# The first batch of a hashed attention with a gated MLP, its hand-written order of work set anew

## The chip, the cores and the metric

The kernel runs on one core of a Trainium2 chip. The metric is the device time of one execution in microseconds, the median of the runs. In the names of the profile, PE is TensorE (matmuls), PEld its weight loads, DVE VectorE, ACT ScalarE, POOL GpSimd, and SP the queue that issues most transfers.

## The reference

Inputs are q, k and v of shape (4 batches, 8 heads, 768 positions, 64), a projection of 64 x 6, and four weight matrices. All is float32.

```python
q_bits = einsum('bhsd,dk->bhsk', q, proj) > 0          # 6 signs for each position
k_bits = einsum('bhsd,dk->bhsk', k, proj) > 0
mask   = (bucket of q_bits)[:, :, :, None] == (bucket of k_bits)[:, :, None, :]
scores = where(mask, q @ k.T / 8, -1e9)
attn   = softmax(scores)                               # with 1e-9 in the denominator
x      = (attn @ v), heads side by side                # 3072 tokens x 512
out    = x + sigmoid(x @ w_res) * ((gelu(x @ w_gate) * (x @ w_val)) @ w_out)
```

The six signs of a position make its bucket number, and a query attends only to keys of its bucket. The MLP widens 512 to 1536.

## The kernel before

**Pairs and chunks.** Two heads of a batch make a pair: p = 0 to 3 in the first batch, 16 in all. The scores of a pair are 768 x 768 for each of two heads; they are cut into nine chunks of 128 x 1024, so that a batch has 36 chunks, "scores 0" to "scores 35". A chunk is three steps. `scores` (line 407) multiplies keys by queries into one of two PSUM buffers `sp`; ScalarE's exponential (line 412) turns it into a bf16 tile `e`; `values` (line 381, "av n" in the order) multiplies `e` by the values and a column of ones and sums into PSUM, eight matmuls of 65 columns. When a head is through, a small matmul (`preset`, line 352) and `finish` (reciprocal and product, lines 332 and 333) give its part of `x_tok`.

**The mask inside the matmul.** Each position's 64 numbers are widened to 71: the 64, six signs of plus or minus one half, and a constant. A match of all six signs adds a large number to the score, and the exponential of the others vanishes. So before a pair's scores its q and k go through these pieces, whose names are those in the order ("1k0" is pair 1, k, head 0):

- `load` (line 78, "ld"; the first pair head by head on line 96, all of them issued by SP).
- "tr": VectorE transposes 32x32 blocks of the loaded tile (line 194).
- "cast": the 64 columns are written in bf16 into one of four tiles `nat` (lines 182, 184 and 186, by engine).
- "hash": fp32 matmuls with the projection. Pair 0 has one piece for each head and side (`hash_one`, line 235). Pair 1 has two pieces over four heads at once, one for each half of the 64 (`hash_heads`, line 253). Pairs 2 and 3 are done together in four pieces (`hashed`, line 206), as are pairs 4 and 5 of the next batch ("hash 4.0" to "hash 4.3").
- "toks": VectorE transposes the sums back to positions (line 259 for pair 1, line 216 for 2 and 3).
- "bits": the signs are written into `nat`, in four instructions of 32 partitions (line 266 for one head of one side, 32x36; line 225 for both heads of one side, 32x72), on VectorE or in turns on GpSimd and VectorE. Pair 0 has its own form on line 243.
- "turn": six transposes on TensorE (line 285) into a PSUM bank, "r" or "f", which `BANK` names.
- "evac": that bank is copied into the tile `aug`, from which scores are made (line 292 on ScalarE, line 294 on VectorE). For pair 0 "a" and "b" are two parts of such a copy.

For the values, "vals_a" copies v in bf16 (line 299) and "vals_s" sums it (lines 307 to 311), both on GpSimd, which also issues the weight loads ("load_w", line 169). "fill" are matmuls on zeros at the start, "spread s" and "spread w" place the projection, and "x 2" transposes a part of `x_tok` for the MLP.

**What sets the order.** No scheduler: every instruction goes to its engine's queue in the order in which the pieces are called, each queue runs in that order, and waits are added where data or a buffer is not ready. For the first batch the pieces stand in one long string, `ORDER`; `WHO` names the engine of a piece where it isn't the default. "work n" issues what a table has for chunk n (loads and values' preparation of the next pairs). After "scores 35" ScalarE loads the table for gelu, the gate and value products of the first batch follow (`gate_val`, lines 426, 445 and 446), with the signs of pairs 4 to 7 between them, and from then on each batch's attention runs in turns with the former batch's output projection (lines 458 and 472). That part isn't touched.

Of the kernel before, what the change touches and what calls it, by code (L numbers as in the profile page):

```python
# [17 lines left out]
def kernel(  # L18
# [20 lines left out]
    T = S // P  # L39
# [24 lines left out]
    e_pool = ctx.enter_context(tc.tile_pool(name="e", bufs=4))  # L64
# [257 lines left out]
    av = {}  # L322
# [207 lines left out]
    def put(name, fn):  # L530
        do[name] = fn

    BANK = {1: "rfrf", 2: "rfrf", 3: "rrfr"}
    G, V, A = nc.gpsimd, nc.vector, nc.scalar
    WHO = {"cast 0k0": A, "cast 0q0": A, "cast 0q1": A, "cast 2k": V, "evac 0k0a": A,
           "evac 0q0": A, "evac 0q1": A, "bits 1q0": (G, V), "bits 1q1": (G, V)}
# [5 lines left out]
    for h in range(2):  # L542
        for e in range(2):
            x = "0%s%d" % ("qk"[e], h)
# [8 lines left out]
            if e == 0:  # L553
                put("evac " + x, lambda h=h, x=x: turned(0, 0, h, WHO.get("evac " + x, V)))
            else:
                put("evac " + x + "a", lambda h=h, x=x: turned(0, 1, h, WHO.get("evac " + x + "a", V), 0, 2))
                put("evac " + x + "b", lambda h=h, x=x: turned(0, 1, h, WHO.get("evac " + x + "b", V), 2, T))
    put("fill b", lambda: fill(2, 256))
    for p in range(1, HP):
        for e in range(2):  # L560
            x = "%d%s" % (p, "qk"[e])
            put("tr " + x, lambda p=p, e=e: tr(p, e))
            put("cast " + x, lambda p=p, e=e, x=x: cast(p, e, WHO.get("cast " + x, G)))
            if p == 1:
                for h in range(2):
                    put("bits %s%d" % (x, h), lambda p=p, e=e, h=h, x=x: bits_head(p, e, h, WHO.get("bits %s%d" % (x, h), ((V,), (G, V))[e])))
            else:
                put("bits " + x, lambda p=p, e=e, x=x: bits(p, e, WHO.get("bits " + x, ((V,), (G, V))[e])))
            for h in range(2):
                y = "%s%d" % (x, h)  # L570
                put("turn " + y, lambda p=p, e=e, h=h, y=y: turn_pe(p, e, h, BANK[p][2 * h + e]))
                put("evac " + y, lambda p=p, e=e, h=h, y=y: turned(p, e, h, WHO.get("evac " + y, V)))
    for i in range(2):
        put("hash 1.%d" % i, lambda i=i: hash_heads(1, i))
    put("toks 1", lambda: tok_heads(1))
    for i in range(4):
        put("hash 2.%d" % i, lambda i=i: hashed((2, 3), i, i + 1))
    put("toks 2", lambda: tokens((2, 3)))
# [60 lines left out]
    def mlp_mm(n):  # L639
# [10 lines left out]
        "tr 0q0, fill a, spread s, hash 0q0, cast 0k0, tr 0k0, cast 0k1, cast 0q0, tr 0q1, "  # L650
        "hash 0k0, bits 0q0, bits 0k0, fill b, turn 0q0, turn 0k0, evac 0q0, tr 0k1, evac 0k0a, "
        "cast 0q1, spread w, hash 0q1, vals_a 0, cast 1k, hash 0k1, cast 1q, "
        "scores 0, tr 1q, evac 0k0b, vals_s 0, bits 0k1, load_v 3, "
        "scores 1, bits 0q1, tr 1k, turn 0k1, "
        "scores 2, turn 0q1, tr 2q, av 0, evac 0k1a, cast 2q, hash 1.0, evac 0q1, evac 0k1b, "
        "scores 3, hash 1.1, av 1, toks 1, bits 1q0, av 2, bits 1k0, "
        "scores 4, bits 1k1, bits 1q1, "
        "scores 5, av 3, turn 1q0, evac 1q0, "
        "scores 6, av 4, vals_a 1, "
        "scores 7, turn 1k0, finish 00, vals_s 1, ld 4q, av 5, evac 1k0, "  # L660
        "scores 8, av 6, load_w 0, tr 2k, "
        "scores 9, tr 3k, tr 3q, av 7, turn 1k1, "
        "scores 10, turn 1q1, evac 1q1, evac 1k1, cast 2k, load_w 1, cast 3k, av 8, "
        "scores 11, ld 4k, cast 3q, av 9, av 10, "
        "scores 12, hash 2.0, vals_a 2, ld 5q, hash 2.1, "
        "scores 13, hash 2.2, hash 2.3, finish 01, av 11, toks 2, "
        "scores 14, av 12, ld 5k, "
        "scores 15, av 13, bits 2q, bits 2k, turn 2q0, "
        "scores 16, evac 2q0, turn 2k0, vals_a 3, work 16, "
        "scores 17, av 14, load_w 2, evac 2k0, finish 10, turn 2q1, vals_s 2, "  # L670
        "scores 18, evac 2q1, av 15, load_w 3, bits 3k, "
        "scores 19, turn 2k1, bits 3q, av 16, av 17, "
        "scores 20, ld 6q, av 18, av 19, evac 2k1, "
        "scores 21, turn 3q0, "
        "scores 22, av 20, ld 6k, evac 3q0, turn 3k0, "
        "scores 23, tr 4q, turn 3q1, evac 3q1, ld 7q, "
        "scores 24, av 21, cast 4k, evac 3k0, av 22, "
        "scores 25, av 23, work 25, "
        "scores 26, cast 4q, vals_s 3, turn 3k1, ld 7k, av 24, "
        "scores 27, tr 5q, evac 3k1, av 25, "  # L680
        "scores 28, tr 5k, tr 4k, cast 5k, work 28, av 26, "
        "scores 29, av 27, cast 5q, tr 7q, "
        "scores 30, hash 4.0, x 2, av 28, tr 6q, "
        "scores 31, hash 4.1, "
        "scores 32, hash 4.2, av 29, "
        "scores 33, hash 4.3, av 30, "
        "scores 34, tr 7k, av 31, tr 6k, work 34, "
# [84 lines left out]
```

## Time and profile before

| | |
|---|---|
| median of 3 runs | 344.62 us (344.42 to 345.3) |
| the profiled execution, its time | 344.05 us |
| its span, first to last instruction | 342.3 us |
| TensorE busy | 337.0 us (98%) |
| ScalarE busy | 208.1 us (61%) |
| VectorE busy | 192.9 us (56%) |
| GpSimd busy | 86.1 us (25%) |
| first exponential of the first batch starts | 9.53 us |
| gelu's table is loaded, after the last exponential of the first batch | 47.07 us |
| granted TensorE clock | 1.00 |

Matmuls are pipelined, so a busy TensorE need not be at its peak: the time from the start of one group to the start of the next says more than the busy share. In a timeline row the columns are the start, the length from the first start to the last end of a merged group, the engine, line and operation, out<-in with shapes and count, and in brackets the idle time of the engine before it with what ended it. Neighbouring instructions of one engine may overlap a little, so a group of n is shorter than n times one.

### The profile page before, as it was taken

The numbers are of one execution on the slowest core, as the hardware profiler recorded it, in microseconds if no ns is written. First come the engines' busy times: TensorE is split into PE (matmuls) and PEld (weight loads), VectorE is DVE, ScalarE is ACT, GpSimd is POOL, SyncE is SP. The second block draws the span as 40 slices with busy tenths as digits, with TensorE's granted clock in tenths as the row PEclk, the third lists the DMA queues.
The fourth block names the chain that finished last, engine by engine and source line by source line (L and its number), as shares of the span: only waits on it lengthen the run. The fifth ranks groups of instructions, "written<-read, shape, count | busy, mean of one in ns | idle before, by whom it ended". The sixth has DMA issues, their size and how long they took to land.

```text
span 342.3 us, 7633 instructions
## 1 busy us (share of the span) xinstructions
PE 337.0 (98%) x3124; PEld 204.6 (60%) x3124; DVE 192.9 (56%) x406; ACT 208.1 (61%) x235; POOL 86.1 (25%) x165
## 2 busy tenths in 40 slices
PE   8999999999999999999999999999999999999995
PEld 5667665665666665655666665656566665665443
DVE  6878847574444876756344775747334444333343
ACT  4889973237999862325999991222999994322220
POOL 3899830370055000170054000242030000000000
PEclk9999999999999999999999999999999999999999
DMA  7979999979386523518467542725431221000012
GB/s 225 377 153 231 308 184 183 162 114 208 123 186 191 159 77 90 110 19 166 105 164 213 181 107 69 132 49 103 82 97 36 56 56 61 3 0 0 33 61 93
DMA packets 69571, 42.50 MB, mean 124 GB/s; under 512 B 47904, under 2 KB 66592, under 8 KB 69536
## 3 DMA queue, kind: packets, MB, share of 16 engines
q1 hardware_dynamic: 63120, 36.77, 42.5%
q0 software_dynamic: 6336, 5.24, 10.6%
q8 instruction: 24, 0.39, 0.5%
q14 instruction: 11, 0.09, 0.1%
q10 hardware_dynamic: 80, 0.00, 0.0%
HBM read 29.36 MB, written 6.29 MB: 104 GB/s over the span
## 4 chain that ended last, share of the span: by engine, by line
PE 94%; ACT 3%; DMA 1%; DVE 1%; issue 0%; SPq 0%; DVEq 0%; ACTq 0%
PE sp L426 37%; PE fps L472 18%; PE sp L407 17%; PE av L381 10%; PE rps L458 6%; PE hs L206 3%; ACT e L412 3%; PE pt L285 1%; DMA ld<-in_q_dram 1%; PE pt L365 1%; PE hs L235 0%; PE av L352 0%; PE hsh L253 0%; PE av L355 0%; DVE o L479 0%
## 5 line engine op out<-in xcount | busy, mean ns | idle before, releaser
L412 ACT ACTIVATE e<-sp 128x1024 bf16<-128x1024 f32 x144 | 143.6, 1026 | 13.1 <-PE sp L407 8.4
L445 ACT ACTIVATE gt<-sp 128x768 bf16<-128x768 f32 x48 | 38.9, 811 | 93.6 <-PE sp L426 93.6
L407 PE MATMUL sp<-aug,aug 71*128 71x256 bf16 (+1 forms) x384 | 85.8, 325 | 0.3 <-ACT e L412 0.2
L472 PE MATMUL fps<-wo,hh 128*128 128x512 bf16 (+2 forms) x300 | 79.3, 370 | 0.0
L446 DVE TENSOR_TENSOR hh<-gt,sp 128x768 bf16<-128x768 bf16 x48 | 45.8, 955 | 52.1 <-PE sp L426 50.0
L426 PE MATMUL sp<-x_sb,wg 128*128 128x512 bf16 (+1 forms) x384 | 70.5, 326 | 0.1
L426 PE MATMUL sp<-x_sb,wv 128*128 128x512 bf16 (+1 forms) x384 | 70.4, 326 | 0.0
L381 PEld LDWEIGHTS <-e 128*128 128x128 bf16 x1152 | 52.7, 97 | 28.9 <-issue 1.2
L381 PE MATMUL av<-va,e 128*128 128x65 bf16 x1152 | 57.6, 193 | 0.0
L426 PEld LDWEIGHTS <-wg 128*128 128x128 bf16 x384 | 37.0, 98 | 26.0 <-issue 1.8
L426 PEld LDWEIGHTS <-wv 128*128 128x128 bf16 x384 | 37.6, 98 | 24.8
L472 PEld LDWEIGHTS <-hh 128*128 128x128 bf16 x300 | 27.5, 97 | 23.2
L407 PEld LDWEIGHTS <-aug 71*128 71x128 bf16 x384 | 29.4, 97 | 10.9 <-issue 1.4
L194 DVE STREAM_TRANSPOSE t<-ld 128x768 f32<-128x768 f32 (+1 forms) x34 | 30.7, 913 | 4.1 <-DMA ld<-in_q_dram 2.2
L307 POOL TENSOR_TENSOR v<-ldv 128x384 f32<-128x384 f32 x16 | 15.9, 996 | 66.5 <-DMA ldv<-in_v_dram 66.5
L184 POOL TENSOR_SCALAR nat<-ld 128x768 bf16<-128x768 f32 x15 | 12.4, 829 | 73.5 <-DMA aug<-nat 73.5
L476 DVE SCALAR_TENSOR_TENSOR o<-th,fps 128x512 f32<-128x512 f32 (+2 forms) x25 | 16.6, 666 | 24.5 <-PE fps L472 20.1
L458 PE MATMUL rps<-wr,x_sb 128*128 128x512 bf16 x96 | 28.1, 378 | 0.0
L332 DVE RECIPROCAL rec<-av 128x6 f32<-128x6 f32 x32 | 6.2, 193 | 32.9 <-PE av L381 31.0
L359 DVE COPY av<-av 128x390 f32<-128x390 f32 x24 | 13.6, 565 | 19.3 <-PE av L355 19.2
L462 ACT ACTIVATE th<-rps 128x512 f32<-128x512 f32 x24 | 14.2, 593 | 16.5 <-PE rps L458 16.5
L225 DVE TENSOR_SCALAR nat<-htp 32x72 bf16<-32x72 f32 x96 | 21.9, 229 | 1.7
(67 smaller groups left out, 209.5 us busy)
## 6 DMA issues: line engine op xcount, KB each, us to landing
ldv<-in_v_dram SPq DMA_DIRECT2D x16, 384.0 KB, 5.1
out_dram<-o SPq DMA_DIRECT2D x23, 256.0 KB, 2.1
ld<-in_q_dram SPq DMA_DIRECT2D x15, 384.0 KB, 5.1
ld<-in_k_dram SPq DMA_DIRECT2D x15, 384.0 KB, 4.5
wg<-in_moe_w_gate_dram POOLq DMA_DIRECT2D x4, 384.0 KB, 6.8
wv<-in_moe_w_val_dram POOLq DMA_DIRECT2D x4, 384.0 KB, 6.8
wo<-in_moe_w_out_dram POOLq DMA_DIRECT2D x3, 512.0 KB, 6.1
wr<-in_moe_w_res_dram POOLq DMA_DIRECT2D x1, 512.0 KB, 11.6
```

What stands on the lines that cost most here:

```text
L194: nc.vector.transpose(t32[p, side][:, sl].rearrange("p c h n -> p (c h n)"), raw[p, side][:, sl].rearrange("p c d -> p (c d)"))
L225: engs[a % len(engs)].tensor_scalar(nat_of(x)[32 * a:32 * a + 32, :, D:D + NBITS], ht[32 * j:32 * j + 32, :, NBITS * a:NBITS * (a + 1)], 0 ...
L307: nc.gpsimd.tensor_add(v3, vs[:, :, 0:3, :], vs[:, :, 3:6, :])
L381: nc.tensor.matmul(av[p, hi][:, qt, :], e[:, off:off + P], va[:, hi, jt, 0:D + 1], start=first, stop=(p >= HP and jt == T - 1), skip_group ...
L407: nc.tensor.matmul(sp[:, off:off + nq * P], ks[0:KA, hi * T + jt, :], qs[0:KA, hi * T + qt0:hi * T + qt0 + nq, :], start=True, stop=True)
L412: nc.scalar.activation(e, sp, AF.Exp, scale=float(ALPHA))
L426: nc.tensor.matmul(sp[:, c0:c1], w[:, kk, bass.ts(m, P)], xs[:, kk, c0:c1], start=(kk == 0), stop=(kk == KM - 1))
L445: nc.scalar.activation(gt, sp[:, 0:S], AF.Gelu)
L446: nc.vector.tensor_mul(hh[:, m, :], gt, ps[1][:, 0:S])
L458: nc.tensor.matmul(rps, x_sb[b][:, kk, t, :], wr[:, kk, :], start=(kk == 0), stop=(kk == KM - 1))
L472: nc.tensor.matmul(fps[:, cs], hh[:, m, bass.ts(t, P)], wo[:, m, cs], start=(m == 0), stop=(m == KF - 1))
L476: nc.vector.scalar_tensor_tensor(o[:, cs], th[:, cs], 1.0, fps[:, cs], op0=ALU.add, op1=ALU.mult)
```

## The change

Only the first batch's order and four tables beside it change; the computation is the same.

- The third and fourth pair (p = 2 and 3) are hashed each by itself, like the second, so that their signs are 32x36 pieces by head. The two hash pieces of a pair now stand together; the four of pairs 4 and 5 stand two and two.
- The first copies of pair 0's q are made in two parts (four of the six blocks, then two), as those of k were.
- Six buffers of `e` instead of four, so that a chunk's values may come up to six chunks behind its scores; in the new order they come up to four behind (av 3 after scores 7), three in the old one (av 29 after scores 32).
- Engines: the cast of 0k0 goes from ScalarE to GpSimd, 0k1 from GpSimd to ScalarE, 1q from GpSimd to ScalarE, 1k and 3q from GpSimd to VectorE, 2k from VectorE to GpSimd; several copies and signs change engine as `WHO` says.
- The order of nearly all pieces before and between the 36 chunks is new, that of loads and weight loads too.

```diff
@@ -61,7 +61,7 @@
     aug_pool = ctx.enter_context(tc.tile_pool(name="aug", bufs=4))
     t32_pool = ctx.enter_context(tc.tile_pool(name="t32", bufs=6))
     va_pool = ctx.enter_context(tc.tile_pool(name="va", bufs=4))
-    e_pool = ctx.enter_context(tc.tile_pool(name="e", bufs=4))
+    e_pool = ctx.enter_context(tc.tile_pool(name="e", bufs=6))
     sm_pool = ctx.enter_context(tc.tile_pool(name="sm", bufs=2))
     sc_ps = ctx.enter_context(tc.tile_pool(name="sc_ps", bufs=2, space=PSUM))
     av_ps = ctx.enter_context(tc.tile_pool(name="av_ps", bufs=2, space=PSUM))
@@ -530,10 +530,12 @@
     def put(name, fn):
         do[name] = fn
 
-    BANK = {1: "rfrf", 2: "rfrf", 3: "rrfr"}
+    BANK = {1: "rffr", 2: "rfrf", 3: "rfrf"}
     G, V, A = nc.gpsimd, nc.vector, nc.scalar
-    WHO = {"cast 0k0": A, "cast 0q0": A, "cast 0q1": A, "cast 2k": V, "evac 0k0a": A,
-           "evac 0q0": A, "evac 0q1": A, "bits 1q0": (G, V), "bits 1q1": (G, V)}
+    WHO = {"cast 0k1": A, "cast 0q0": A, "cast 0q1": A, "cast 1k": V, "cast 1q": A, "cast 3q": V,
+           "evac 0k0a": A, "evac 0k0b": A, "evac 0k1b": A, "evac 0q0a": A, "evac 0q0b": A,
+           "evac 0q1b": A, "evac 2k1": A, "bits 1k1": (G,), "bits 1q1": (G, V), "bits 2k0": (G,),
+           "bits 2k1": (V,), "bits 2q1": (G, V), "bits 3k1": (G,), "bits 3q0": (G, V)}
     put("fill a", lambda: (fill(7), fill(1, 256)))
     put("spread s", lambda: spread(
         lambda a: projs[32 * a:32 * a + 32, :, 32 * a:32 * a + NBITS], (G, A, A, G)))
@@ -551,7 +553,8 @@
             else:
                 put("turn " + x, lambda e=e, h=h: turn_pe(0, e, h))
             if e == 0:
-                put("evac " + x, lambda h=h, x=x: turned(0, 0, h, WHO.get("evac " + x, V)))
+                put("evac " + x + "a", lambda h=h, x=x: turned(0, 0, h, WHO.get("evac " + x + "a", V), 0, 4))
+                put("evac " + x + "b", lambda h=h, x=x: turned(0, 0, h, WHO.get("evac " + x + "b", V), 4, T))
             else:
                 put("evac " + x + "a", lambda h=h, x=x: turned(0, 1, h, WHO.get("evac " + x + "a", V), 0, 2))
                 put("evac " + x + "b", lambda h=h, x=x: turned(0, 1, h, WHO.get("evac " + x + "b", V), 2, T))
@@ -561,21 +564,14 @@
             x = "%d%s" % (p, "qk"[e])
             put("tr " + x, lambda p=p, e=e: tr(p, e))
             put("cast " + x, lambda p=p, e=e, x=x: cast(p, e, WHO.get("cast " + x, G)))
-            if p == 1:
-                for h in range(2):
-                    put("bits %s%d" % (x, h), lambda p=p, e=e, h=h, x=x: bits_head(p, e, h, WHO.get("bits %s%d" % (x, h), ((V,), (G, V))[e])))
-            else:
-                put("bits " + x, lambda p=p, e=e, x=x: bits(p, e, WHO.get("bits " + x, ((V,), (G, V))[e])))
             for h in range(2):
                 y = "%s%d" % (x, h)
+                put("bits " + y, lambda p=p, e=e, h=h, y=y: bits_head(p, e, h, WHO.get("bits " + y, ((V,), (G, V))[e])))
                 put("turn " + y, lambda p=p, e=e, h=h, y=y: turn_pe(p, e, h, BANK[p][2 * h + e]))
                 put("evac " + y, lambda p=p, e=e, h=h, y=y: turned(p, e, h, WHO.get("evac " + y, V)))
-    for i in range(2):
-        put("hash 1.%d" % i, lambda i=i: hash_heads(1, i))
-    put("toks 1", lambda: tok_heads(1))
-    for i in range(4):
-        put("hash 2.%d" % i, lambda i=i: hashed((2, 3), i, i + 1))
-    put("toks 2", lambda: tokens((2, 3)))
+        for i in range(2):
+            put("hash %d.%d" % (p, i), lambda p=p, i=i: hash_heads(p, i))
+        put("toks %d" % p, lambda p=p: tok_heads(p))
     for p in range(HP):
         put("vals_a %d" % p, lambda p=p: vals_a(p))
         put("vals_s %d" % p, lambda p=p: vals_s(p))
@@ -647,44 +643,46 @@
 
 
     ORDER = (
-        "tr 0q0, fill a, spread s, hash 0q0, cast 0k0, tr 0k0, cast 0k1, cast 0q0, tr 0q1, "
-        "hash 0k0, bits 0q0, bits 0k0, fill b, turn 0q0, turn 0k0, evac 0q0, tr 0k1, evac 0k0a, "
-        "cast 0q1, spread w, hash 0q1, vals_a 0, cast 1k, hash 0k1, cast 1q, "
-        "scores 0, tr 1q, evac 0k0b, vals_s 0, bits 0k1, load_v 3, "
-        "scores 1, bits 0q1, tr 1k, turn 0k1, "
-        "scores 2, turn 0q1, tr 2q, av 0, evac 0k1a, cast 2q, hash 1.0, evac 0q1, evac 0k1b, "
-        "scores 3, hash 1.1, av 1, toks 1, bits 1q0, av 2, bits 1k0, "
-        "scores 4, bits 1k1, bits 1q1, "
-        "scores 5, av 3, turn 1q0, evac 1q0, "
-        "scores 6, av 4, vals_a 1, "
-        "scores 7, turn 1k0, finish 00, vals_s 1, ld 4q, av 5, evac 1k0, "
-        "scores 8, av 6, load_w 0, tr 2k, "
-        "scores 9, tr 3k, tr 3q, av 7, turn 1k1, "
-        "scores 10, turn 1q1, evac 1q1, evac 1k1, cast 2k, load_w 1, cast 3k, av 8, "
-        "scores 11, ld 4k, cast 3q, av 9, av 10, "
-        "scores 12, hash 2.0, vals_a 2, ld 5q, hash 2.1, "
-        "scores 13, hash 2.2, hash 2.3, finish 01, av 11, toks 2, "
-        "scores 14, av 12, ld 5k, "
-        "scores 15, av 13, bits 2q, bits 2k, turn 2q0, "
-        "scores 16, evac 2q0, turn 2k0, vals_a 3, work 16, "
-        "scores 17, av 14, load_w 2, evac 2k0, finish 10, turn 2q1, vals_s 2, "
-        "scores 18, evac 2q1, av 15, load_w 3, bits 3k, "
-        "scores 19, turn 2k1, bits 3q, av 16, av 17, "
-        "scores 20, ld 6q, av 18, av 19, evac 2k1, "
-        "scores 21, turn 3q0, "
-        "scores 22, av 20, ld 6k, evac 3q0, turn 3k0, "
-        "scores 23, tr 4q, turn 3q1, evac 3q1, ld 7q, "
-        "scores 24, av 21, cast 4k, evac 3k0, av 22, "
-        "scores 25, av 23, work 25, "
-        "scores 26, cast 4q, vals_s 3, turn 3k1, ld 7k, av 24, "
-        "scores 27, tr 5q, evac 3k1, av 25, "
-        "scores 28, tr 5k, tr 4k, cast 5k, work 28, av 26, "
-        "scores 29, av 27, cast 5q, tr 7q, "
-        "scores 30, hash 4.0, x 2, av 28, tr 6q, "
-        "scores 31, hash 4.1, "
-        "scores 32, hash 4.2, av 29, "
-        "scores 33, hash 4.3, av 30, "
-        "scores 34, tr 7k, av 31, tr 6k, work 34, "
+        "fill a, spread s, cast 0k0, tr 0q0, tr 0k0, tr 0q1, hash 0q0, spread w, cast 0q0, "
+        "hash 0k0, fill b, bits 0q0, turn 0q0, cast 0q1, bits 0k0, cast 1q, hash 0q1, evac 0q0a, "
+        "tr 0k1, evac 0q0b, turn 0k0, vals_a 0, bits 0q1, tr 1q, hash 0k1, evac 0k0a, evac 0k0b, "
+        "cast 0k1, ld 4k, "
+        "scores 0, vals_s 0, load_v 3, "
+        "scores 1, bits 0k1, cast 1k, tr 1k, turn 0k1, turn 0q1, evac 0q1a, "
+        "scores 2, vals_a 1, tr 2q, av 0, av 1, evac 0k1b, "
+        "scores 3, hash 1.0, hash 1.1, cast 2q, cast 2k, evac 0k1a, toks 1, av 2, bits 1k0, "
+        "bits 1q0, evac 0q1b, bits 1q1, "
+        "scores 4, "
+        "scores 5, bits 1k1, turn 1k0, "
+        "scores 6, tr 2k, turn 1q0, evac 1q0, "
+        "scores 7, evac 1k0, av 3, av 4, finish 00, load_w 0, "
+        "scores 8, load_w 1, av 5, load_w 2, "
+        "scores 9, turn 1q1, tr 3q, turn 1k1, "
+        "scores 10, evac 1k1, av 6, vals_s 1, av 7, evac 1q1, "
+        "scores 11, vals_a 2, ld 4q, av 8, "
+        "scores 12, cast 3q, cast 3k, finish 01, av 9, av 10, "
+        "scores 13, hash 2.0, hash 2.1, tr 3k, toks 2, bits 2k1, "
+        "scores 14, bits 2k0, av 11, "
+        "scores 15, av 12, ld 5q, load_w 3, bits 2q1, av 13, "
+        "scores 16, turn 2k0, bits 2q0, av 14, av 15, vals_s 2, evac 2k0, work 16, turn 2q0, "
+        "scores 17, av 16, evac 2q0, turn 2k1, "
+        "scores 18, turn 2q1, finish 10, evac 2q1, "
+        "scores 19, vals_a 3, ld 5k, av 17, ld 6k, evac 2k1, hash 3.0, hash 3.1, "
+        "scores 20, toks 3, bits 3q0, ld 6q, ld 7q, bits 3k0, "
+        "scores 21, av 18, bits 3q1, cast 4q, turn 3q0, "
+        "scores 22, tr 4k, av 19, evac 3q0, av 20, bits 3k1, "
+        "scores 23, av 21, turn 3k0, "
+        "scores 24, evac 3k0, turn 3q1, vals_s 3, "
+        "scores 25, tr 4q, tr 5q, tr 5k, work 25, turn 3k1, "
+        "scores 26, av 22, "
+        "scores 27, av 23, av 24, "
+        "scores 28, evac 3k1, evac 3q1, work 28, ld 7k, av 25, av 26, "
+        "scores 29, av 27, "
+        "scores 30, hash 4.0, hash 4.1, "
+        "scores 31, tr 6k, cast 4k, av 28, av 29, "
+        "scores 32, tr 6q, hash 4.2, cast 5q, hash 4.3, "
+        "scores 33, x 2, tr 7q, tr 7k, "
+        "scores 34, av 30, cast 5k, work 34, av 31, "
         "scores 35, av 32, av 33"
     )
     chunk = {}
```

## The prediction

> **What bounds the kernel now.** I read the page first, then the timelines of ScalarE, TensorE, VectorE and GpSimd over the first 52 us, then the transfers issued there. From the page:
>
> ```profile
> span 342.3 us, 7633 instructions
> PE 337.0 (98%) x3124; PEld 204.6 (60%) x3124; DVE 192.9 (56%) x406; ACT 208.1 (61%) x235; POOL 86.1 (25%) x165
> ...
> PE 94%; ACT 3%; DMA 1%; DVE 1%; issue 0%; SPq 0%; DVEq 0%; ACTq 0%
> ```
>
> TensorE bounds the whole, but the change touches only the first batch, where ScalarE's 36 exponentials (one per chunk) fill the time nearly as well. What counts is when the last of them ends, since all that follows keeps its order. The timeline of ScalarE (start, duration, name, count, idle before):
>
> ```profile
> 3.78 0.94 ACT L182 ACTIVATE nat<-ld 128x384 bf16<-128x384 f32 x2
> 7.27 1.08 ACT L292 ACTIVATE aug<-pt 71x768 bf16<-71x768 bf16 x2 [2.55 <-PE pt L285]
> 8.24 0.52 ACT L182 ACTIVATE nat<-ld 128x384 bf16<-128x384 f32 x1
> 9.53 2.85 ACT L412 ACTIVATE e<-sp 128x1024 bf16<-128x1024 f32 x3 [0.77 <-PE sp L407]
> 12.26 0.81 ACT L292 ACTIVATE aug<-pt 71x768 bf16<-71x768 bf16 x1
> ...
> 24.85 5.64 ACT L412 ACTIVATE e<-sp 128x1024 bf16<-128x1024 f32 x6 [0.55 <-PE sp L407]
> 30.82 10.30 ACT L412 ACTIVATE e<-sp 128x1024 bf16<-128x1024 f32 x11 [0.34 <-PE sp L407]
> 41.62 2.03 ACT L412 ACTIVATE e<-sp 128x1024 bf16<-128x1024 f32 x2 [0.49 <-PE sp L407]
> ```
>
> Exponentials follow each other every (10.30 - 1.03)/10 = 0.92 us. From the first (9.53) to the last (two from 45.11, so 46.03) are 36.5 us: 35 x 0.92 = 32.2, one PSUM copy (12.26 to 12.95) 0.7, and about 3.6 of waiting, always for scores (line 407). The list of waits names no exponential that waits for a values matmul; a buffer `e` was never short.
>
> How a wait comes about: there are two score buffers, so scores n start at the earliest when exponential n-2 has ended, 1.07 us after that one's start (scores at 10.60, exponential at 9.53); exponential n starts 0.63 us after scores n do (14.31 against 13.68). 2 x 0.92 - 1.07 - 0.63 leaves 0.14 us of play. A chunk's scores occupy TensorE 0.43 us, so other work of 0.92 - 0.43 + 0.14 = 0.63 us fits between two chunks; what is beyond it, ScalarE waits. Prices of that other work, start to start in the timeline of TensorE: values of a chunk 0.25, six transposes 0.34, hash groups as follows.
>
> ```profile
> 23.11 0.86 PE L206 MATMUL hs<-t,projw 128*32 128x192 f32 x16
> 23.90 0.42 PE L381 MATMUL av<-va,e 128*128 128x65 bf16 x8
> ...
> 42.45 0.53 PE L206 MATMUL hs<-t,projw 128*32 128x192 f32 x8
> 42.92 0.42 PE L381 MATMUL av<-va,e 128*128 128x65 bf16 x8
> ```
>
> A hash piece alone takes 0.56 with its entry from the scores (scores at 41.92, their end at 42.35, next work at 42.92); a group of two pieces 0.90 (22.57 + 0.43 = 23.00 to 23.90).
>
> **1. The start: 0.65 later.** ScalarE's new order before the first exponential: casts of 0q0 and 0q1, the cast of 1q, copies of q in two parts, of k in two parts, cast of 0k1. The cast of 1q waits for its load, and the queue is in order, so the first copy (7.27 before) waits with it. That load is the fifth that SP issues, in both kernels, at 2.67, and the view of transfers says
>
> ```profile
> ld<-in_q_dram SPq DMA_DIRECT2D x1, 384.0 KB, 4.7
> ```
>
> so it lands at 7.4. A cast of 768 columns does not occur on ScalarE before. Bounds: 0.72 us of its queue (the 811 ns of `gt`, also 768 columns, less the 0.09 by which neighbours overlap) and 0.86 (two casts of 384, 0.43 start to start). I take 0.80, near the casts. The copies: 768 + 256 columns take 0.97 (7.27 to 8.24), the new 1536 columns 1.46. Cast of 0k1: 0.43. First exponential: 7.45 + 0.80 + 1.46 + 0.43 + 0.04 (a semaphore) = 10.18 against 9.53. TensorE isn't later: its first scores need the first part of k, 7.45 + 0.80 + 0.97 x 1.2 = 9.41, and the exponential could go 0.63 later, at 10.04. Range of this term 0.57 to 0.71.
>
> [...]
>
> The split of the copies hides nothing new, since both parts are on ScalarE ahead of the first exponential. That VectorE is spared its 0.41 us copy at 8.39 gains nothing: its next users wait for hashes.
>
> **2. Copies between exponentials: 0.75 later.** Now three: second part of 0k1 (512 columns, 0.49), second part of 0q1 (256, 0.26), 2k1 (768, 0.70), 1.45 in all, for one of 0.70 before. All stand in the exponentials' own queue; only where ScalarE would wait anyway do they cost nothing (see 20 below).
>
> **3. Hash pieces together: waits of 3.6 become 2.45.** Three groups fewer, each 2 x 0.56 - 0.90 = 0.22 of TensorE. What matters is where they fall. By the rule of 0.63, with what the timeline shows before, new figures in order:
> - exponential 4: waited 0.45 (a hash piece and two chunks of values ahead of scores 4). Now a group and one chunk of values, but the exponentials themselves come later by 0.65 + 0.49, so nothing: 0.
> - 11: 0.25 before, behind transposes, values and a preset (0.34 + 0.25 + 0.17). Now two chunks of values stand there (0.50): 0.
> - 13 and 14: two groups of 0.90 in neighbouring slots, waits 0.41 and 0.65. Now the third pair's group alone, behind scores 13: 0.90 - 0.63 plus some lateness, 0.4.
> - 17 and 18: new, 0.85, worked out below.
> - 20: 0.44 before. The fourth pair's group falls here, but ScalarE copies 2k1 just then: 0 beside the 0.70 already counted.
> - 31 to 34: four lone pieces, waits 0.62, 0.09, 0.33, 0.33. Now two groups: 0.90 - 0.63 = 0.3 and, behind two chunks of values, 0.5.
> - small ones of 0.05 to 0.1: 0.4.
>
> **The new wait at 17.** The third pair's signs are now made head by head in 32x36 pieces: 16 instructions a pair, where two pairs together had 16 of 32x72, and those of 2k0 are all on GpSimd. From GpSimd's timeline:
>
> ```profile
> 14.11 3.16 POOL L266 TENSOR_SCALAR nat<-hth 32x36 bf16<-32x36 f32 x8
> ```
>
> with the next start at 17.34, so 0.40 each. On TensorE the transposes of 2k0 stand after scores 16, and behind them values 14 and 15, the transposes of 2q0 and scores 17. If scores 13 start at time t, the group ends at t + 0.43 + 0.90, with its drain 0.25 and the transpose to tokens 0.38 the signs start at t + 2.0, GpSimd is through at t + 3.65, and then come 0.34 + 0.50 + 0.34 and 0.63 to exponential 17: t + 5.5. Undisturbed it would start at t + 0.7 + 4 x 0.92 + the 0.4 at 14 = t + 4.8. So 0.7, and 0.15 more at 18, where the copy of 2q0 is late. GpSimd must be free by then: 14.5 + eight signs 3.2 + three weight issues (0.98, 0.89, 0.85 in this trace) + sums 2.05 + values copy 0.95 + cast 0.82 = 24.2, and the signs want it at about 24.3. Just so; its cover is nil.
>
> [...]
>
> **4. What I put at nothing.** The buffers of `e` and values further behind: no exponential waited for them; they let 3 happen. Loads: 4k and 4q issue earlier, 5q and 5k follow the first transposing DMA of `x_sb` (22.5 before), those of pairs 6 and 7 the second (31.5, as before); 12 us and 9 us later their transposes read them, and the longest landing of these early loads is 8.5. The cast of 0k0 goes to GpSimd, which is idle from 3.6 to 6.1 and needs 0.50. The banks r and f alternate in both orders. The third weight slice (46.4) comes some 2 us later and is wanted six gate blocks after 46.4, at 2.45 each near 61. VectorE takes two casts instead of one and about 0.5 us more of signs; it idles over 6 us of these 38. TensorE idles 0.8 us before the first scores; the granted clock is 1.00 throughout, so I price no slow matmuls.
>
> **Sum.** 0.65 + 0.75 + (2.45 - 3.6) = +0.25 us. The profiled execution took 344.05 around its span of 342.3; it becomes 344.3. The median of the runs is 0.57 above it: 344.62 + 0.25 = 344.9.
>
> **Rivals.**
> - Slower, decided at GpSimd's signs of the third pair. If GpSimd finishes its cast of 3k after 24.3, every microsecond is one at scores 17, and ScalarE has nothing later to make it good. With the 0.55 of its 32x72 signs in place of 0.40, twelve signs (eight of the second pair, four of these) give 12 x 0.15 = 1.8: 344.9 + 1.8 = 346.7; half of it 345.8. For it: zero cover, signs of both engines at once. Against: the same form measured 0.40 beside VectorE.
> - Faster: neither the start nor 17 waits. If the load of 1q came 0.65 earlier and the signs were ready with the transposes, 0.65 + 0.85 go: 343.4. Against: the loads ahead of it are unchanged and 4.7 us is measured.
> - It does nothing: the exponentials are paced by scores alone, and moved work only changes which slot waits: 344.6. For it: both engines have under 4 us of slack, and my terms nearly cancel.
>
> **How the numbers follow.** A measurement of this kernel tells 0.3%, 1.03 us, from no change. My sum and the third rival lie within it: 0.62 together (0.47 and 0.15). The slower rival and mishaps on its path beyond 1.03: 0.24. The faster rival: 0.14. Range: without the wait at 17 and with the low start price, 344.9 - 0.85 - 0.1, and a little toward the faster rival, 343.6; above, three quarters of the GpSimd rival, 346.2.
>
> **What would show it.** First exponential near 10.2, behind a ScalarE cast that waits for a load; a wait of 0.7 before the 18th; last exponential starting near 46.3. The prediction is wrong if the first exponential starts by 9.6, if exponential 17 waits not at all or over 1.5 us, or if the stages after 48 us change in length.

## The result and the profile after

The changed kernel takes 345.40 us (median of 22 runs, 344.70 to 348.86) against 344.49 for the one before (22 runs, 343.93 to 345.30): a ratio of 1.0031, 95% interval 1.002 to 1.0042. It is slower by 0.91 us; forecast were 0.25 more, 344.9, with a range of 343.6 to 346.2. The difference lies under the 1.03 us that the prediction takes for the limit of one measurement; over 22 runs the interval still excludes no change.

The profiled execution of the changed kernel is the one of 348.86 us, so it must be read with care. From its page, beside the lines shown of before:

```profile
span 347.1 us, 7643 instructions
PE 339.9 (98%) x3124; PEld 206.6 (60%) x3124; DVE 192.8 (56%) x412; ACT 210.1 (61%) x240; POOL 87.9 (25%) x173
...
PEclk9679999999999999999999999999999999999999
...
PE 92%; ACT 3%; DMA 2%; SPq 0%; DVE 0%; issue 0%; DVEq 0%; ACTq 0%
```

The second and third digit of PEclk are new (before had 9 throughout), and so is the 1% more of DMA on the chain that ended last. ScalarE's timeline shows both (start, length, engine, line, operation, shapes, count, idle before):

```profile
5.06 0.52 ACT L182 ACTIVATE nat<-ld 128x384 bf16<-128x384 f32 x1 [0.81 <-DMA ld<-in_q_dram]
8.24 0.84 ACT L182 ACTIVATE nat<-ld 128x768 bf16<-128x768 f32 x1 [2.65 <-DMA ld<-in_q_dram]
8.99 1.60 ACT L292 ACTIVATE aug<-pt 71x512 bf16<-71x512 bf16 x4
10.47 0.53 ACT L182 ACTIVATE nat<-ld 128x384 bf16<-128x384 f32 x1
10.88 1.94 ACT L412 ACTIVATE e<-sp 128x1024 bf16<-128x1024 f32 x2
...
17.59 1.94 ACT L412 ACTIVATE e<-sp 128x1024 bf16<-128x1024 f32 x2 [1.56 <-PE sp L407]
19.99 1.02 ACT L412 ACTIVATE e<-sp 128x1024 bf16<-128x1024 f32 x1 [0.47 <-PE sp L407]
21.49 1.02 ACT L412 ACTIVATE e<-sp 128x1024 bf16<-128x1024 f32 x1 [0.47 <-PE sp L407]
```

The cast of 1q holds ScalarE for 2.65 us, until its load lands at 8.24 (7.41 in the profile before, issued at 2.67 in both). Then exponentials follow each other only every 1.5 us. TensorE's timeline and its table by stretches say why (in the table: stretch, its length, busy time of PE, PEld, DVE, ACT and POOL with counts, granted clock, DMA share, GB/s):

```profile
7.67 0.87 PE L235 MATMUL hs<-t,projs 128*128 128x192 f32 x4
10.16 1.04 PE L407 MATMUL sp<-aug,aug 71*128 71x512 bf16 x5 [1.62 <-ACT aug L292]
...
18.20 0.85 PE L285 MATMUL pt<-ident,nat 128*71 128x128 bf16 x6
```

```profile
0.00:11.90 11.90, 9.21 (x55) 6.04 (x56) 8.85 (x24) 6.62 (x14) 5.19 (x20) 1.00 0.79 256
11.90:22.10 10.20, 10.15 (x82) 6.26 (x81) 5.92 (x16) 7.28 (x10) 7.72 (x18) 0.50 0.74 244
22.10:46.00 23.90, 23.60 (x366) 17.10 (x365) 20.05 (x50) 22.59 (x25) 19.74 (x42) 1.00 1.09 233
```

After 1.62 us without work TensorE's granted clock fell to one half from 11.9 to 22.1; six transposes take 0.85 there, 0.50 to 0.53 elsewhere. From first to last exponential this run needs 39.61 us, and the same order at full clock 36.48 (below): 3.1 us. But it is one run of 22; the others have a mean clock of 0.997 to 1.0, and half clock for 3.41 us (a third of this stretch) would already give 0.995 (an estimate, over 347 us). The half clock explains the slowest run, not the median.

### The profile page after: what moved, and what is told of

It is laid out like the page before. It is cut to its first block, busy times and chain, and to the rows that moved or that the text cites. A ratio compares the mean times of both kernels' runs of the same rounds, so it can differ in the third digit from the quotient of the medians.

```text
span 347.1 us, 7643 instructions
## 1 busy us (share of the span) xinstructions
PE 339.9 (98%) x3124; PEld 206.6 (60%) x3124; DVE 192.8 (56%) x412; ACT 210.1 (61%) x240; POOL 87.9 (25%) x173
## 4 chain that ended last, share of the span: by engine, by line
PE 92%; ACT 3%; DMA 2%; SPq 0%; DVE 0%; issue 0%; DVEq 0%; ACTq 0%
PE sp L426 36%; PE fps L472 18%; PE sp L407 18%; PE av L381 10%; PE rps L458 6%; PE hs L206 2%; ACT e L412 2%; DMA ld<-in_q_dram 2%; PE pt L285 1%; PE hsh L253 1%; ACT aug L292 1%; PE pt L365 1%; SPq L96 0%; PE av L352 0%; ACT nat L182 0%
## 5 line engine op out<-in xcount | busy, mean ns | idle before, releaser
L407 PE MATMUL sp<-aug,aug 71*128 71x256 bf16 (+1 forms) x384 | 88.3, 334 | 1.7 <-ACT aug L292 1.6
L184 POOL TENSOR_SCALAR nat<-ld 128x768 bf16<-128x768 f32 x13 | 11.6, 891 | 73.8 <-DMA aug<-nat 73.7
```

Source lines behind the costliest of these rows:

```text
L407: nc.tensor.matmul(sp[:, off:off + nq * P], ks[0:KA, hi * T + jt, :], qs[0:KA, hi * T + qt0:hi * T + qt0 + nq, :], start=True, stop=True)
```

## The experiments

All kernels from here on are stand-ins: the transposing DMAs are replaced by plain copies, and later batches' scores use the first batch's q and k, so the later batches' result is left out. The stand-in of after takes as long as after itself, 345.42; that of before takes 1.0 us more than before. Steps that wait for no load repeat within 0.02 us between profiles of one order; the landing of loads does not repeat (that of 1q, issued in its place, came between 6.97 and 8.24). "Exponential n" is the start of the n-th, and a step is the time from one start to the next, both read from the single instructions.

```diff
-        ag = aug_pool.tile([P, HT, P], BF16, tag=f"aug{side}", name=f"aug{side}")
-        nc.sync.dma_start_transpose(out=ag, in_=nat_of(x).rearrange("p c n -> p (c n)"))
+        ag = aug[p % HP, side]
+        nc.sync.dma_start(ag[KA:P].rearrange(...), nat_of(x)[KA:P].rearrange(...))
```

**The two orders at full clock.**

> A stand-in for the kernel before, as a basis for the experiments: its 35 transposing DMAs are replaced by plain copies on the same queue at the same places. Those of x_tok copy it as it is; those of pairs 4 to 15 copy the unused rows of nat into the unused rows of the first batch's transposed tiles, and the later batches take q and k from the first batch. So the later batches' result is left out, while the instructions of every compute engine are those of the kernel before, in its order. Expected by every theory: the first batch as before (first exponential 9.5, last one 46.0), a time within 1 us of 344.5.

> The same stand-in for the changed kernel. Expected by every theory: 0.9 us above the stand-in for the kernel before, as the changed kernel is above it. Theory of the start: its first exponential starts past 10.1, behind ScalarE's cast of 1q that waits for its load, and this is most of the 0.9 us. Theory of the slots: the first exponential is late by 0.65 at most and waits between the exponentials make the rest. Theory of the clock: TensorE's granted clock falls to 0.50 for a stretch after its idle time ahead of the first scores, as in the first profile of the changed kernel (0.50 from 11.9 to 22.1 us after 1.62 us of idling), and typical runs pay for that in part.

Measured: stand-in of before 345.5 (345.25 to 345.78), ratio to before 1.0032 (1.0019 to 1.0044); of after 345.42 (344.47 to 346.2), 1.0028 (1.0019 to 1.0038). In the former the values of pair 0 reached GpSimd at 9.35 instead of 8.56, and step 6 was 1.49 instead of 0.90, a wait for signs; the other 0.4 lies behind exponential 35 (296.68 against 296.31), where before's profile is the shortest of all. So the stand-in of after is compared with the profile of before itself, at clock 1.00 both:

| | before | prediction's change | stand-in of after | measured change |
|---|---|---|---|---|
| load of 1q landed | 7.41 | 0 | 6.97 | -0.44 |
| exponential 0 | 9.53 | +0.65 | 9.61 | +0.08 |
| 0 to 4 | 4.78 | -0.40 | 4.46 | -0.32 |
| 4 to 6 | 1.83 | 0 | 1.82 | -0.01 |
| 6 to 14 | 8.71 | -0.91 | 7.82 | -0.89 |
| 14 to 18 | 3.70 | +0.85 | 5.17 | +1.47 |
| 18 to 30 | 11.53 | +0.26 | 11.95 | +0.42 |
| 30 to 35 | 5.95 | -0.57 | 5.26 | -0.69 |
| behind 35 | 296.31 | 0 | 296.62 | +0.31 |

(The prediction's 0.4 of small waits has no place of its own.) From 0 to 35 before took 36.50 and after 36.48: all that is gained up to 14 and behind 30 is used up between, most of it at exponential 17. The 0.31 behind 35 falls almost all in the last 55 us, in the stand-in of before as well (54.58 there, 54.59 here, 54.27 before), so it isn't taken for the change's. What is left is the start.

**Does the start hang on that load?** Cast of 1q taken off ScalarE in after, and put there in before:

```diff
-"cast 1q": A, ... bits 0k0, cast 1q, hash 0q1 ... tr 2q, av 0
+             ... bits 0k0, hash 0q1 ... tr 2q, cast 1q, av 0        # on VectorE
```

> The stand-in for the changed kernel with one cast moved: 1q goes to VectorE, behind tr 2q, so that nothing on ScalarE waits for that load ahead of the first copies. Theory of the start: the first exponential starts near 9.5 and the end moves by as much, 0.6 to 1.3 us down from the stand-in for the changed kernel. Theory of the slots: what is won at the start is lost in the waits after it, 0.2 at most is left. Theory of the clock: TensorE's idle time ahead of the first scores falls under 0.6 us and the clock stays at 1.00.

> The stand-in for the kernel before with one part of the change: the cast of 1q on ScalarE ahead of the first copy, where it waits for its load. Theory of the start: the first exponential moves from 9.5 to 10.1 or later; the end is later by 0.4 to 1.0 us, as some is given back by GpSimd's relief and by waits that the delay covers. Theory of the slots: under 0.3 later.

```diff
-load(1, 0); load_v(0); load(1, 1)
+load_v(0); load(1, 1); load(1, 0)
```

> The stand-in of after with the load of 1q issued two places later on SP, behind the values of pair 0 and behind 1k, so that it lands near 9.5 instead of 7.0 to 8.2. ScalarE's cast of 1q then holds the first copies, the first exponential should start near 12.1 (landing + 2.64), and TensorE idles some 3 us before the first scores. Theory clock (TensorE idle for 1.6 us or more there is followed by a granted clock of one half for several windows of 3.4 us): rows of 0.50 in the windows after 12 us, steps of 1.5 in place of 0.95 between early exponentials, 3 to 4 us beyond the late start; time 349 to 351. Rival start (a late load only shifts the start): clock 1.00, first exponential 2.5 later, and part of it covered by later waits; time 346.5 to 347.9.

Measured: 345.45 (345.42 to 345.63), 345.34 (344.59 to 346.38) and 349.21 (347.31 to 350.56). ScalarE's timeline of the last:

```profile
9.42 0.84 ACT L182 ACTIVATE nat<-ld 128x768 bf16<-128x768 f32 x1 [3.54 <-DMA ld<-in_q_dram]
10.17 1.60 ACT L292 ACTIVATE aug<-pt 71x512 bf16<-71x512 bf16 x4
11.65 0.53 ACT L182 ACTIVATE nat<-ld 128x384 bf16<-128x384 f32 x1
12.06 2.85 ACT L412 ACTIVATE e<-sp 128x1024 bf16<-128x1024 f32 x3
```

In every profile with after's order the first exponential starts 2.64 after the cast of 1q: 6.97 and 9.61, 7.57 and 10.22, 8.24 and 10.88, 9.42 and 12.06. And lateness is handed on whole: with starts at 9.61 and 12.06 exponentials 0 to 35 took 36.48 each. Earliness is not: with the cast on VectorE the start was 9.29, but the stretch took 37.49, since VectorE's copies and GpSimd's signs came later (step 4 1.79, step 6 1.05). GpSimd's timeline in the stand-in of after, then with the cast on VectorE:

```profile
8.10 0.82 POOL L299 CAST va<-ldv 128x768 bf16<-128x768 f32 x1 [2.88 <-DMA ldv<-in_v_dram]
...
14.00 3.20 POOL L266 TENSOR_SCALAR nat<-hth 32x36 bf16<-32x36 f32 x8
```

```profile
8.63 0.82 POOL L299 CAST va<-ldv 128x768 bf16<-128x768 f32 x1 [3.34 <-DMA ldv<-in_v_dram]
...
14.53 3.20 POOL L266 TENSOR_SCALAR nat<-hth 32x36 bf16<-32x36 f32 x8
```

So a second chain hangs on the next load of SP's queue, the values of pair 0: from their copy to its signs of pair 1 GpSimd needs 5.90 both times, hardly pausing, and exponential 6 comes 7.79 after that copy both times. The copy starts 1.11 to 1.15 after the landing of 1q in the five profiles that show both. By that, 8.63 stands for a landing at 7.50 (an estimate), and the cast on ScalarE would have given 7.50 + 2.64 + 6.28 = 16.42 for exponential 6 (6.28 is the stretch from 0 to 6 in the stand-in of after), which is where it came without it. The two chains are level, and taking the cast away shortens only one.

In before's order the cast on ScalarE cost 0.59 at the start (10.08) and 0.21 at exponential 35; as the copy of the values started at 9.35 without it and at 8.70 with it, the 0.21 is not its price at equal loads. Neither median moved as the theory of the start had it (345.45 against 345.42, 345.34 against 345.5).

**Does the idle stretch halve the clock?** Zeros on TensorE ahead of the first scores, with the late load:

```diff
-hash 0k1, evac 0k0a
+hash 0k1, fill c, evac 0k0a          # fill c: ten matmuls of 512 columns on zeros
```

> As the kernel with the late load of 1q, and ten matmuls on zeros (512 columns each, about 0.21 us at full clock) behind the hash of 0k1 on TensorE, so that it idles about 1 us instead of 3 before the first scores, which don't come later by that. Theory clock: the granted clock stays 1.00, steps of early exponentials are 0.95 again, and the time is 346.5 to 347.9, 3 us less than without the zeros. Rival (the clock does not hang on that idle stretch): same clock and same time as without the zeros.

Measured 348.08 (347.77 to 349.16). With the late load alone the four runs had mean clocks of 0.999, 0.995, 0.99 and 0.985 at 347.31, 348.87, 349.55 and 350.56: 3.25 us over 1.4%, or 1.2 for each half per cent. A third of after's stretch at half clock, 3.41 us, would be 0.5% of the span (an estimate). But a later landing lengthens both the idle stretch (none with the landing at 6.97, 1.62 at 8.24, 2.03 at 9.42) and the time, and the landings of these runs aren't known, so not all of the 3.25 need be the clock's. With the zeros the clocks were 1.0, 1.0, 0.998 and 0.995, and the median missed the 346.5 to 347.9 that was expected. Both profiles show 1.00 in the whole first batch (0.999 and 1.0 over the span); in the one with zeros 1q landed at 10.64, 1.2 later than in the other, so their times can't be set against each other. Three runs of four with lost clock against one or two speak for the theory, but don't show it; what the zeros gain stays open.

**Who is late at exponential 17?** One piece moved in GpSimd's queue:

```diff
-scores 12, cast 3q, cast 3k, finish 01 ... evac 2q1,
+scores 12, cast 3q, finish 01 ... evac 2q1, cast 3k,        # behind scores 18
```

> The stand-in of after (transposing DMAs replaced by plain copies, so that the later batches' result is left out), with one piece moved: GpSimd's cast of 3k goes from behind scores 12 to behind scores 18, so that it no longer stands ahead of the third pair's four signs in GpSimd's queue. In the stand-in of after that cast ended at 24.22 while the tokens were ready at 23.52, and exponential 17 waited 1.41 (step 2.33). Theory GpSimd (its lateness sets the wait at 17): the signs start about 0.7 earlier, the step at 17 falls to 1.6, and the last exponential comes 0.7 earlier; time 344.7 against 345.4. Rival hash (the chain from the hash group through tokens and signs sets it): the step at 17 stays above 2.2 and the time at 345.4. Rival slots (time won at 17 is lost again in later waits): step 17 near 1.6, but the steps from 18 to 35 give it back, time 345.3.

Measured 345.11 (344.39 to 345.92), ratio 1.0018 (1.0007 to 1.0028). GpSimd's timeline in the stand-in of after, and below it TensorE's:

```profile
23.41 0.81 POOL L186 CAST nat<-ld 128x768 bf16<-128x768 f32 x1
24.32 1.61 POOL L266 TENSOR_SCALAR nat<-hth 32x36 bf16<-32x36 f32 x4
```

```profile
25.98 0.53 PE L285 MATMUL pt<-ident,nat 128*71 128x128 bf16 x6 [0.59 <-POOL nat L266]
```

GpSimd's timeline with the cast of 3k moved:

```profile
23.97 0.14 POOL L300 MEMSET va<- 128x12 bf16 x1
24.30 1.53 POOL L266 TENSOR_SCALAR nat<-hth 32x36 bf16<-32x36 f32 x4 [0.19 <-DVE hth L259]
```

In the first the cast ends at 24.22, the tokens were ready at 23.52, and the transposes of 2k0 wait. In the second GpSimd waits for the tokens; the step at 17 falls from 2.33 to 1.63, and the stretch from 0 to 35 from 36.48 to 35.77. The 0.7 is GpSimd's and lasts to the end; the median gains 0.31, and which landings its runs had isn't recorded. After's own profile shows the same from the other side: at half clock the hash came late, GpSimd idled 1.56 before these signs, and the step at 17 was 1.62.

**Hash pieces together, alone** (in the stand-in of before):

```diff
-cast 2q, hash 1.0, evac 0q1, evac 0k1b, scores 3, hash 1.1, av 1
+cast 2q, evac 0q1, evac 0k1b, scores 3, hash 1.0, hash 1.1, av 1
-scores 30, hash 4.0, ... scores 31, hash 4.1, scores 32, hash 4.2, av 29, scores 33, hash 4.3
+scores 30, ... scores 31, hash 4.0, hash 4.1, scores 32, av 29, scores 33, hash 4.2, hash 4.3
```

> The stand-in of before with one part of the change alone: the two hash pieces of pair 1 stand together behind scores 3, and the four of pairs 4 and 5 stand two and two behind scores 31 and 33. By the prediction's prices the waits at 31 to 34 fall from 1.37 to 0.8 and the one at 4 from 0.45 to about 0.6, since both pieces now stand ahead of scores 4. Theory slots (a group of two costs 0.22 less than two alone and the exponentials gain what TensorE saves): last exponential 0.4 to 0.5 earlier than in the stand-in of before, time 345.0 against 345.5. Rival nothing: the wait only changes its slot, time 345.5. A time above 345.8 speaks against both.

Measured 344.76 (344.04 to 345.25), ratio 1.0006 (0.9996 to 1.0017), 0.74 below the stand-in of before (in the profiles 0.30 of that is an earlier start, 9.19 against 9.49). ScalarE's timeline with the pieces apart, then together:

```profile
42.17 2.03 ACT L412 ACTIVATE e<-sp 128x1024 bf16<-128x1024 f32 x2 [0.49 <-PE sp L407]
44.42 1.02 ACT L412 ACTIVATE e<-sp 128x1024 bf16<-128x1024 f32 x1 [0.22 <-PE sp L407]
45.67 1.94 ACT L412 ACTIVATE e<-sp 128x1024 bf16<-128x1024 f32 x2 [0.23 <-PE sp L407]
```

```profile
42.54 1.94 ACT L412 ACTIVATE e<-sp 128x1024 bf16<-128x1024 f32 x2 [0.30 <-PE sp L407]
44.79 1.94 ACT L412 ACTIVATE e<-sp 128x1024 bf16<-128x1024 f32 x2 [0.31 <-PE sp L407]
```

Waits of 0.3 twice (the prices were 0.3 and 0.5) in place of four; exponentials 30 to 35 took 5.47 instead of 5.97. Step 4 fell too, 1.37 to 1.22.

**Can both costs be taken away?** Cast of 1q on GpSimd and 2k's behind scores 8; then also 3k's and two weight issues behind scores 18:

```diff
-bits 0k0, cast 1q, hash 0q1 ... scores 0, vals_s 0 ... cast 2q, cast 2k ... scores 8, load_w 1
+bits 0k0, hash 0q1 ... scores 0, cast 1q, vals_s 0 ... cast 2q ... scores 8, cast 2k, load_w 1
```

> The stand-in of after with the cast of 1q taken off ScalarE and given to GpSimd, behind the copy of pair 0's values, so that the first exponential no longer hangs on the landing of 1q; to keep GpSimd's signs of pair 1 in time, its cast of 2k goes from behind scores 3 to behind scores 8. Theory start (from exponential 0 to exponential 35 the stand-ins of after with the first exponential at 9.61, 12.06 and 13.29 all took 36.48, so a start earlier is an end earlier, one for one): first exponential at 9.2 to 9.5, last one 36.5 later at 45.9, and a median 0.5 to 0.9 below the 345.4 of after's stand-in: 344.6 to 344.9. Rival cover (what is won at the start is waited for later, as when the cast went to VectorE, where 36.48 became 37.49): last exponential at 46.5 or later, time 345.4.

> As the kernel with the cast of 1q on GpSimd, and the third pair's signs freed too: GpSimd's cast of 3k goes behind scores 18, and so do its third and fourth weight issue, which stood ahead of and between the third pair's signs. Theory start and GpSimd together (they add: 0.9 at the start, 0.7 at exponential 17): first exponential at 9.2 to 9.5, step at 17 of 1.6, last exponential at 45.1, median 343.8 to 344.2, below both kernels (344.5 and 345.4). Rival (only one of the two gains lasts): 344.6 to 344.9. Rival weights (the weight slices now come too late for the first gate blocks): last exponential at 45.1 and yet a time above 344.6, with the stage behind 46 us longer than in after's stand-in.

Measured 346.05 (345.64 to 346.69) and 345.7 (344.78 to 347.75): slower than after's stand-in. Two more, set by those traces: 2q's cast behind the signs too, and the weight issues at scores 25; and, with GpSimd as it was but for 3k, the cast of 1q on ScalarE ahead of exponential 4.

```diff
-evac 0q1b, bits 1q1
+evac 0q1b, cast 1q, bits 1q1        # the second of the two; cast 1q gone from ahead of hash 0q1
```

> As the kernel with both moves on GpSimd (cast of 1q there, cast of 3k behind scores 18), with two things set right that its trace named: the cast of 2q goes behind GpSimd's signs of pair 1, since the transposes of 1k0 waited 0.58 for those signs (step at exponential 6 1.29 in place of 0.90), and the third and fourth weight issue go to scores 25, since exponential 22 waited 0.7 for the signs of 3k0 behind them (step 1.63). Theory GpSimd (what was won at the start was lost only where GpSimd's queue came late): signs of pair 1 start 0.7 earlier, steps at 6 and 22 fall to 0.90 and 0.95, step 17 stays 1.63, last exponential near 45.5, median 344.0 to 344.4. Rival loads (the landings of 1q, the values and 1k set when the signs of pair 1 can be made, whichever engine is free): exponential 6 not before 16.3 and last one at 46.1 or later; median 344.8 to 345.5.

> The stand-in of after with GpSimd's cast of 3k behind scores 18, and the cast of 1q still on ScalarE but later, behind the second part of 0q1's copy and ahead of exponential 4, so that no work ahead of the first exponentials waits for the load of 1q, and GpSimd has nothing more to do. Theory start (only the hang on the landing costs): first exponential at 9.2 to 9.5, 0.75 of cast ahead of exponential 4, of which up to 0.4 hides under the wait that pair 1's signs make at 6; exponential 6 near 16.3, step 17 at 1.6, last exponential near 45.8, median 344.2 to 344.6 with less scatter than the 344.4 to 345.9 of the kernel with 3k moved alone. Rival loads (a start before the loads allow is waited for at 6): exponential 6 near 16.5 in any case, last one at 46.0 or later, median 344.9 to 345.2.

Measured 344.64 (343.67 to 345.33), ratio 0.9999 (0.9986 to 1.0011), and 344.84 (344.46 to 345.86), 1.0013 (1.0002 to 1.0024). TensorE's timeline, cast on GpSimd alone:

```profile
16.30 0.53 PE L285 MATMUL pt<-ident,nat 128*71 128x128 bf16 x6 [1.36 <-DVE nat L266]
```

and with GpSimd's queue set anew:

```profile
15.03 0.53 PE L285 MATMUL pt<-ident,nat 128*71 128x128 bf16 x6 [0.65 <-POOL nat L266]
```

These are the transposes of 1k0. Starts were at 9.42, 9.80, 9.22 and 9.32; exponential 6 came at 17.36, 16.52, 16.08 and 16.39 (15.89 in after's stand-in): pair 1's signs, not the first exponential, set the pace there, and they hang on the values of pair 0, whose copy started at 9.74, 8.91, 9.17 and 8.73 (8.10 in after's stand-in). The four kernels got 0 to 35 in 38.80, 37.04, 36.93 and 36.57. Step 17 was 2.82, 1.62, 2.06 and 1.62; the second lost its gain at exponential 22 (step 1.63 in place of 0.95, signs of 3k0 behind the weight issues), which the third mended. The fourth pays for the cast at exponential 4 (step 1.90 in place of 1.27). All four medians lie above what the theory gave. Part of that is loads: after's own order, with a copy of the values as late, would end 37.99 behind it (46.09 less 8.10; an estimate), and against this the last exponentials of the four come 0.49 later, then 0.06, 1.01 and 0.83 earlier. Their medians, against 345.42, lie 0.63 and 0.28 higher, 0.78 and 0.58 lower. The third is 0.8 below after's stand-in and level with before; none beats both kernels clearly.

## Why the prediction was right or wrong

The time lay in the range and on the right side of no change, but 0.5 above the sum. One term was clearly mis-sized, the wait at 17 (3 and 4); one was near, but stood on a landing that doesn't repeat (1).

1. **The start.** Price of the cast (0.80) and order were right: it measured 0.84, of which 0.75 is queue time. At the landing of 7.41 the rule of 2.64 gives 10.05, so +0.52 and not +0.65, just under the bound of 0.57. What failed is "so it lands at 7.4": a fixed landing, taken from one execution. In the four profiles with this cast on ScalarE and the load in its old place it landed at 6.97, 7.57, 7.57 and 8.24. Lateness goes to the end one for one, since 36.48 followed the starts at 9.61, 12.06 and 13.29. At 7.41 the last exponential would come at 10.05 + 36.48 = 46.53, 0.50 behind before's 46.03; against the stand-in of before, at its later loads, the same sum gives 0.75 (both estimates). The medians differ by 0.91. The rest is open: runs without a profile don't show their landings, and the stretch behind 35 alone took 296.31 to 297.12 over the profiles.
2. **Copies between exponentials and waits up to 14** were right: -0.40 and -0.91 predicted, -0.32 and -0.89 measured.
3. **The wait at 17** was mis-sized: 0.7 predicted, 1.41 at full clock. The 0.7 is what the chain through hash, tokens and signs costs alone (step 1.63 with 3k moved). "Just so; its cover is nil" was the point that decided: GpSimd came free at 24.22, as worked out (24.2), but the tokens were there at 23.52 and not at 24.3, and the 0.70 that it was late is the 0.70 more at exponential 17. The drain of 0.25 in that chain stands in no row: the transpose to tokens began 0.14 after the work behind the hash group on TensorE in before (23.90 to 24.04), 0.13 in the stand-in of after (23.01 to 23.14). A later start doesn't mend it: the step was 2.33 with the late load as well, for the reason under 4. So the slower rival's mechanism holds, with 0.7 in place of 0.9 to 1.8; its price was wrong in kind, since the signs kept their 0.40 and the lateness came from the queue ahead of them.
4. **VectorE beside GpSimd.** VectorE's ten signs took 2.59 (1.95 with 3k moved), and the transposes of 2k0 waited 0.59 for GpSimd's signs, not for these. But the change also gave VectorE the cast of 3q, and that lengthened a GpSimd addition ahead of the signs. Of GpSimd in after's stand-in, the addition beside that cast, and a later one without:

```profile
20.12 1.41 POOL L307 TENSOR_TENSOR v<-ldv 128x384 f32<-128x384 f32 x1
...
27.72 0.99 POOL L307 TENSOR_TENSOR v<-ldv 128x384 f32<-128x384 f32 x1
```

and of VectorE:

```profile
20.13 0.55 DVE L184 TENSOR_SCALAR nat<-ld 128x768 bf16<-128x768 f32 x1
```

   With the late load GpSimd reached that addition 0.52 sooner after the first exponential, and it took that much longer:

```profile
22.05 1.94 POOL L307 TENSOR_TENSOR v<-ldv 128x384 f32<-128x384 f32 x1
```

```profile
22.58 0.55 DVE L184 TENSOR_SCALAR nat<-ld 128x768 bf16<-128x768 f32 x1
```

   In seven of the eight stand-ins in which the two overlap, the addition ends 0.85 or 0.86 after the cast does, whenever it began; in the eighth the cast took 1.17 instead. So it is VectorE's new cast that fixes when GpSimd comes to the signs, and with the late load less work ahead of the addition won nothing. Of GpSimd's 0.70 it makes 0.42 in the stand-in of after; with the late load it makes 0.95, without which GpSimd would have come before the tokens and the 0.7 of the sum would have held (worked out from the rows; no run takes the cast of 3q off VectorE). The failed step is the one that put VectorE's second cast at nothing. In six of the eight the addition had begun first and was still the one that took longer (1.41 and 1.94 in the rows above, 0.99 without the cast beside it); what holds it up, no run shows.
5. **31 to 34** were right: two waits of 0.3 in the stand-in of before; 30 to 35 -0.69 against -0.57 in after's.
6. **"I price no slow matmuls"** was wrong as a rule, though it hardly moves the median: it costs 3.1 us in the run where it happens.
7. What else was put at nothing (buffers, later loads, weights) shows no wait of an exponential. The "does nothing" rival is near in outcome and wrong in reason: the stretch from 0 to 35 is 36.48 against 36.50 because +1.89 (14 to 30) and -1.91 (the other stretches) cancel. That is luck, and so is part of the hit: the start at 7.41 (0.13 less than priced), 30 to 35 (0.12 less) and the 0.4 of small waits, for which the other stretches leave about 0.25, stand against 0.62 more at 14 to 18.

The stated marks: exponential 0 near 10.2 behind a ScalarE cast (10.88 and 9.61, the latter just above the 9.6 that would have spoken against it), a wait of 0.7 at exponential 17 and not over 1.5 (1.41), last exponential near 46.3 (46.09 in the stand-in, 50.49 at half clock), stages after 48 us unchanged (gelu's table to the end within 0.35 us).

## What to carry to other kernels

Don't put work that waits for a late load ahead of the first work on the engine that paces the stage: the load's scatter then becomes the kernel's, one for one (starts at 9.61, 12.06 and 13.29 were each followed by 36.48 us to the last exponential). TensorE's idle time may cost its clock too: in one profiled run the granted clock was 0.50 for 10.24 us after 1.62 us of it, in another 2.03 us left it at 1.00. When a step's cover is worked out as nil, take its lateness into the sum, and follow the whole queue ahead of it, with what the change puts beside it on other engines. An engine that starts earlier gains only up to the next thing that hangs on the same loads; compare profiles at equal landings.

## What was not expected of the hardware

- TensorE's granted clock fell to 0.50 for 10.24 us (11.9 to 22.1) after 1.62 us of idleness (8.54 to 10.16), having been at 1.00 for 6.83: three and two times 3.41. In other executions 2.03 and 1.43 us left it at 1.00. So the length of the idle stretch alone doesn't decide; what does, no run here shows.
- The same 384 KB load, fifth on the same queue and issued at 2.67 in the two profiles that show it, landed at 7.41 and 8.24; over the five profiles that show it there, between 6.97 and 8.24.
- VectorE's cast of 1k (768 columns) took 0.55 in the stand-in of after, where an addition of GpSimd had 0.10 us left, and 1.31 in after itself, where one had 0.89 left.
